# Summing the taps of a shift convolution and joining filter spectra with accumulating transfers

## The chip, the cores and the metric

The kernel runs on one core of a Trainium2 chip. The metric is the device time of one execution in microseconds (us). The core has five instruction queues that matter here: TensorE (PE) for matrix products, VectorE (DVE), ScalarE (ACT), GpSimd (POOL) and SyncE (SP), which only issues transfers. Each works through its own instructions in order and waits on semaphores that other engines and transfers raise. POOL issues transfers too, in a queue of its own.

## What is computed

S = 2048 positions, D = 640 channels, F = 1536. With x = A_q, the reference comes down to this:

```
g  = sigmoid(sum(x * gate_w))                                   # one gate per position
ks = sum over t < 4 of  k_pad[:, t:t+S, :] * shift_k[:, 3-t]    # shift convolution: 4 taps
kv = ks * v
y  = irfft(rfft(kv, 2S) * rfft(ssm_k, 2S))[:S] + kv * ssm_D     # long convolution per channel
a  = q * y
h  = layernorm(x);  u = gelu(einsum("bsd,sf->bdf", h, w1) + b1)
b  = transpose(einsum("bdf,fs->bds", u, w2) + b2)               # MLP over the positions
out = g * a + (1 - g) * b
```

## The kernel before

**The long convolution** is done in P = 4 blocks of 512 positions. Each block of the filter is turned to the time-by-channel layout (`w_time`), transformed to a spectrum `W0..W3` by products with cosine and sine tables on PE (`w_freq`), and evicted from PSUM by ACT with a scale. A spectrum has 9 rows of 640 columns: rows 0 to 3 and 5 to 8 are the cosine and sine parts of four groups of frequencies (`fi`), row 4 holds a copy for the frequency at the edge (`w_nyq`, L1008). Neighbouring spectra are joined (`w_comb`, L998): W_i becomes W_i plus W_(i-1) in frequency groups 2 and 3, and W_i minus W_(i-1) in groups 0 and 1, by two DVE operations over 2560 columns each. Each of the blocks of kv (`kvb`) is folded (`a_split`, into `es`) and transformed into `A0..A3` (`a_freq`). Output block m_ is the sum over j of A_j times W_(m_-j) (`pair`, on DVE, in `Z` with `tT` as scratch), followed by the inverse transform on PE with the table `TI` (`inverse`) and by `epilogue`, which turns half of it round with the matrices `flip` and `flipn`, multiplies by q and the gate and adds the MLP's part.

**The shift convolution** works on tiles of 128 positions, four to a block (`kv_two`). A tile `k4` holds four shifted copies of k side by side, 4 x 640 columns, loaded by one transfer from SP. DVE multiplies it by `shkb`, the taps spread over all partitions (one operation, 2560 columns). PE sums the four products with 4 x 2 accumulating matmuls against the identity, or against `flip` for the two tiles of a block that are stored turned round; ACT evicts the sum to `kvb` and DVE multiplies it by v. For the two turned tiles v is first turned by PE and evicted by ACT. There are four buffers for k4 and five for v.

**The MLP** runs on PE beside this: 384 matmuls `h,w` for the first layer, in blocks of 16 and 32 that hold a PSUM slot, and 384 `gT,w` for the second. Its weights come in pieces by transfers that POOL issues (`w1_load`, `w2_load`). A piece may be loaded only when PE has finished with the buffer's last contents, and for that POOL waits. There are four PSUM slots.

**What sets the order.** Nothing is issued as it is written. Each operation is recorded in a plan with a cost, its reads and writes, and a priority number; `_Plan.run` (L384) then takes, for whichever engine can start earliest, the ready operation of best priority, and this gives the order of each engine's queue. For a transfer the plan uses bytes over a rate and 2 us. `_Tracker` (L18) puts in the waits. So a change of an operation, its engine or its planned cost can move any other operation, and an engine's queue, once set, is kept. Lines named in the profile are mostly those of helpers: L290 every matmul, L676 DVE's two-input operations, L718 ACT's operations, L258 every transfer.

In the function lines, the parts that matter: `dma` (L722) records a transfer, `_Tracker.dma` (L246) issues it; `kv_tile` is L1027, `a_freq` L1043, `tabs` L1111, `inverse` L1114, and the calls in their order are from L1171.

Of the kernel before, what the change touches and what calls it, by code (L numbers as in the profile page):

```python
# [8 lines left out]
BF16 = mybir.dt.bfloat16  # L9
F32 = mybir.dt.float32  # L10
I32 = mybir.dt.int32
ACT = mybir.ActivationFunctionType
# [5 lines left out]
class _Tracker:  # L18
# [227 lines left out]
    def dma(self, stream, out_ap, in_ap, semname, noncontig=False, accum=False):  # L246
        reads = [in_ap]
        writes = [out_ap]
        acc = self.pre(stream, reads, writes)
        engobj = self.eng[stream]  # L250
        sem = self.dma_sems[semname]
        if accum:
            ins = engobj.dma_start(out_ap, in_ap, accum_op=ALU.add)
        elif noncontig:
            with self.nc.allow_non_contiguous_dma(reason="tiny"):
                ins = engobj.dma_start(out_ap, in_ap)
        else:
            ins = engobj.dma_start(out_ap, in_ap)  # L258
        ins.then_inc(sem, 16)
        self.dma_cnt[semname] += 16  # L260
        v = self.dma_cnt[semname]
        self.dma_hist[(semname, v)] = dict(self.known[stream])
        src = ("dma", semname, v)
        for reg, mode in acc:
            self.add_record(reg, mode, src)
        return v
# [250 lines left out]
def _build(nc, A_q, A_k, A_v, A_shift_k, A_ssm_k, A_ssm_D, B_x, B_w1, B_b1, B_w2, B_b2, gate_w, out):  # L517
# [15 lines left out]
    with ExitStack() as es:  # L533
# [14 lines left out]
        def buf(name, shape, dtype, t0, t1):  # L548
            spec.append((name, list(shape), dtype, t0, t1))
# [35 lines left out]
        buf("AFc", [128, 1024], BF16, 0, 90)  # L585
        buf("AFs", [128, 1024], BF16, 0, 90)
        buf("TI", [128, 2, 4, n // 2], BF16, 0, END)
        buf("h", [128, NT, D], BF16, 0, 80)
        groups = [[0], [1]] + [[t, t + 1] for t in range(2, NT, 2)]
        for i in range(2):  # L590
# [83 lines left out]
        def tt(out_, in0, in1, op, pr, eng="DVE"):  # L674
            c = 0.07 + nel(out_) / 1920.0 if eng == "DVE" else 0.3 + nel(out_) / 500.0
            return vop(eng, c, lambda e: e.tensor_tensor(out_, in0, in1, op), [in0, in1], [out_], pr)  # L676
# [16 lines left out]
        def memset(ap, val, pr, eng="POOL"):  # L693
            return vop(eng, 0.3 + nel(ap) / 2000.0, lambda e: e.memset(ap, val), [], [ap], pr)

        def act(out_, in_, func, pr, bias=None, scale=None, accum=None, ps=(), after=()):
            kw = {}
            rr = [in_]
            k = 0
            if bias is not None:  # L700
                kw["bias"] = bias
                if isinstance(bias, bass.AP):
                    rr.append(bias)
                    k += 1
            if scale is not None:
                kw["scale"] = scale
                if isinstance(scale, bass.AP):
                    rr.append(scale)
                    k += 1
            ww = [out_]  # L710
            if accum is not None:
                kw["accum_out"] = accum
                ww.append(accum)
            c = 0.17 + nel(out_) / 1150.0 + 0.09 * k + (0.2 if accum is not None else 0)

            def f(e):
                src = in_() if callable(in_) else in_
                return e.activation(out_, src, func, **kw)  # L718

            return vop("ACT", c, f, rr, ww, pr, ps=ps, after=after)  # L720

        def dma(out_ap, in_ap, semname, pr, stream="SP", noncontig=False):  # L722
            if semname not in T.dma_sems:
                T.add_dma_sem(semname, es.enter_context(nc.semaphore(f"d_{semname}")))
            tot = mybir.dt.size(out_ap.dtype)
            for st, ct in list(out_ap.ap):
                tot *= ct

            def emit():
                T.dma(stream, out_ap, in_ap, semname, noncontig=noncontig)  # L730

            return plan.add(stream, 1.2 if stream == "POOL" else 0.5, emit, [in_ap], [out_ap], pr, dma=max(tot, 20000) / 1e6)

        def pe(pslist, mms, pr, after=()):
            reads = []
# [11 lines left out]
        def two(p_):  # L747
            return lambda: pp[p_.slot][:, :].rearrange("p (c f) -> p c f", c=2)[:, :, 0:HD]
# [4 lines left out]
        def h2(ap):  # L753
            return ap.rearrange("p (c f) -> p c f", c=2)
# [200 lines left out]
        def w_freq(i, pr):  # L955
            osrc = b[f"wT{i}"]
            W = b[f"W{i}"]
            for fi in ORD:
                for c in range(2):
                    p_ = transform(b[f"ee{i % 2}"], osrc, fi, c, pr)  # L960
                    act(h2(W[:, 5 * c + fi, :]), two(p_), ACT.Copy, 1, scale=c_w if fi == 3 else 2.0 / N2, ps=[p_])

        for i in range(P):
            w_time(i)
# [32 lines left out]

        def w_comb(i, pr):  # L998
            W, V = b[f"W{i}"], b[f"W{i - 1}"]


            def half(t, f):
                return bass.AP(tensor=t, offset=f * D, ap=[[9 * D, 128], [5 * D, 2], [1, 2 * D]])

            tt(half(W, 2), half(W, 2), half(V, 2), ALU.add, pr)
            tt(half(W, 0), half(W, 0), half(V, 0), ALU.subtract, pr)

        def w_nyq(i):  # L1008
            W = b[f"W{i}"]
            dma(W[:, 4, :], W[:, 3, :], f"wn{i}", 17)  # L1010
            dma(W[0:1, 4, :], W[0:1, 8, :], f"wn{i}", 17)
            memset(W[0:1, 8, :], 0.0, 2)

        def kv_load(t, pr):
            nm = f"k4_{t % KR}"
# [11 lines left out]
        def kv_tile(t, pr):  # L1027
            k4 = b[f"k4_{t % KR}"]
            v_ = b[f"v_{t % VR}"][:, :]
            r_ = t % NB  # L1030
            mat = b["ident" if r_ < 2 else "flip"][:, :]
            kb = b[f"kvb{t // NB % KVB}"][:, r_ if r_ < 2 else 5 - r_, :]
            if r_ >= 2:
                p_ = _PS()
                pe([p_], halves(p_, [(mat, v_)]), 1.1)
                act(h2(v_), two(p_), ACT.Copy, 1, ps=[p_])
            tt(k4[:, :, :], k4[:, :, :], b["shkb"][:, :, :], ALU.mult, pr)
            p_ = _PS()
            pe([p_], halves(p_, [(mat, k4[:, j, :]) for j in range(KS)]), 1.1)
            act(h2(kb), two(p_), ACT.Copy, 1, ps=[p_])  # L1040
            tt(kb, kb, v_, ALU.mult, pr - 2)

        def a_freq(j, pr):  # L1043
            A = b[f"A{j}"]
            es_ = b["es0"]
            for fi in ORD:
                for c, tab in ((0, AFc), (1, AFs)):
                    p_ = _PS()
                    e0 = 0 if (fi >= 2) == (c == 0) else 2
                    pairs = [(tf(tab, nb, fi), es_[:, e0 + nb, :]) for nb in range(2)]  # L1050
                    pe([p_], halves(p_, pairs), pr)
                    act(h2(A[:, c, fi, :]), two(p_), ACT.Copy, 1, ps=[p_])

        def kv_two(i):
            for t in range(NB * i, NB * i + NB):
# [52 lines left out]
                act(h2(b[f"o1_{q}"][:, k, :]), two(p_), ACT.Identity, 3, bias=b["c2"][:, sb:sb + 1],  # L1108
                    scale=b["omg"][:, sb:sb + 1], ps=[p_])

        def tabs(c, fi, i):  # L1111
            return TI[:, c, fi, i * 128:(i + 1) * 128]

        def inverse(m_):  # L1114
            Z = b[f"Z{m_ % 2}"]
            res = [_PS() for _ in range(4)]
            part = (((0, 2), (0, 3), (1, 0), (1, 1)), ((1, 2), (1, 3), (0, 0), (0, 1)))
            if z_split(m_):
                for i in range(2):
                    for k, fi in enumerate(ORD):  # L1120
                        mms = []
                        for g in range(2):
                            c = [c_ for c_, f_ in part[g] if f_ == fi][0]
                            for h_ in range(2):
                                mms.append((res[2 * i + g], h_ * 512, HD, tabs(c, fi, i),
                                            Z[:, c, fi, h_ * HD:(h_ + 1) * HD], k == 0, k == 3))
                        pe([res[2 * i], res[2 * i + 1]], mms, 1.0)
            else:
                for i in range(2):
                    for g in (1, 0):  # L1130
                        pairs = [(tabs(c, fi, i), Z[:, c, fi, :]) for c, fi in sorted(part[g], key=lambda x: x[1])]
                        pe([res[2 * i + g]], halves(res[2 * i + g], pairs), 1.0)
            return res

# [56 lines left out]
        ts(b["gg"][:, :], b["gth"][:, :], 0.5, 0.5, ALU.mult, ALU.add, 20, eng="POOL")  # L1191
        ts(b["omg"][:, :], b["gth"][:, :], -0.5, 0.5, ALU.mult, ALU.add, 20, eng="POOL")
        tt(b["c2"][:, :], b["omg"][:, :], b["bf"][:, FT:FT + NT], ALU.mult, 20, eng="POOL")
        for q in range(NO):
            mlp2(q)
        for m_ in range(P):
# [37 lines left out]
```

## Time and profile before

| | us |
|---|---|
| median of 3 runs | 226.09 (223.95 to 227.66) |
| span of the profiled execution, first to last instruction | 222.4 |
| PE busy | 202.8 |
| DVE busy | 201.8 |
| ACT busy | 139.9 |
| POOL busy | 41.5 |
| transfers: 39.88 MB, mean over the span | 179 GB/s |

The page gives no time of its own for the profiled execution beside its span; the span is 3.7 us below the runs' median. Busy times count the instructions' own time; an engine that waits isn't busy, and issuing transfers doesn't count for SP. Matmuls overlap, so that the mean of one in the groups is its time from start to end and more than it costs PE. A transfer's "us to landing" runs from its issue to its semaphore.

Stages, by the order of time: filter transforms until about 45 us on PE, with the layernorm's statistics on DVE; from 42 to 126 us the tap products, their sums, the first MLP layer and the first output blocks; from 153 us the second MLP layer on PE beside the last two blocks of `pair` on DVE, the last of which ends at 210.

### The profile page before, as it was taken

Reading aid. Unit: us, or ns where it says so; the run is one execution under the profiler, and the core shown is the slowest. Engines: PE = TensorE matmul, PEld = TensorE weight load, DVE = VectorE, ACT = ScalarE, POOL = GpSimd, SP = SyncE. Lnnn points to the kernel's source line nnn. Section 1 sums busy time; section 2 is a strip of 40 time slices with the busy share of each in tenths; the row PEclk is TensorE's granted clock in tenths of the full one; section 3 lists DMA queues with packets and bytes.
Section 4 is the critical chain, followed back from the end, with each engine's and each line's share of the span. In section 5 each row is a group of like instructions: output and inputs, shape, how many; then the busy total and the mean of one; then the engine's idle time right before and its main releaser. Section 6 shows DMA issues by size and latency. Waiting matters only on the chain.

```text
span 222.4 us, 3751 instructions
## 1 busy us (share of the span) xinstructions
PE 202.8 (91%) x1481; PEld 141.1 (63%) x1481; DVE 201.8 (91%) x253; ACT 139.9 (63%) x221; POOL 41.5 (19%) x79
## 2 busy tenths in 40 slices
PE   0829799999998998999999999999999999999991
PEld 0725547567675774777777777667777777767651
DVE  3379999899988998999999999999999999999771
ACT  4899988997579869683746511799431845432251
POOL 8563330301131010015171010000101101110000
PEclk9988999999999999999999999999999999999997
DMA  6999996139915894899962114302065845286003
GB/s 180 359 325 349 235 298 244 43 109 304 347 41 146 297 391 160 287 295 294 288 181 58 36 16 140 119 3 59 0 202 169 244 116 180 83 253 200 0 3 118
DMA packets 22087, 39.88 MB, mean 179 GB/s; under 512 B 1715, under 2 KB 17205, under 8 KB 22069
## 3 DMA queue, kind: packets, MB, share of 16 engines
q1 hardware_dynamic: 18964, 28.10, 39.8%
q0 software_dynamic: 3104, 11.54, 17.9%
q8 instruction: 12, 0.20, 0.4%
q14 instruction: 7, 0.05, 0.1%
HBM read 36.35 MB, written 2.62 MB: 175 GB/s over the span
## 4 chain that ended last, share of the span: by engine, by line
PE 60%; DVE 22%; ACT 11%; DMA 5%; issue 1%; DVEq 0%; SPq 0%
PE pp L290 60%; DVE Z L676 10%; DVE tT L676 7%; DMA k<-in_A_k_dram 3%; ACT wT L718 2%; ACT W L718 2%; DMA wnat<-in_A_ssm_k_dram 2%; ACT L718 1%; DVE es L676 1%; DVE cg L676 1%; ACT kvb L718 1%; DVE kvb L676 1%; DVE k L676 1%; DVE xg L676 1%; ACT TFs L718 1%
## 5 line engine op out<-in xcount | busy, mean ns | idle before, releaser
L290 PE MATMUL pp<-h,w 128*128 128x320 bf16 x384 | 54.9, 299 | 0.0
L290 PE MATMUL pp<-gT,w 128*128 128x320 bf16 x384 | 53.1, 299 | 0.0
L676 DVE TENSOR_TENSOR tT<-A,W 128x640 bf16<-128x640 bf16 (+4 forms) x44 | 48.0, 1121 | 0.3
L676 DVE TENSOR_TENSOR Z<-Z,tT 128x2560 bf16<-128x2560 bf16 (+3 forms) x35 | 47.1, 1370 | 0.1
L290 PEld LDWEIGHTS pp<-gT,w 128*128 128x128 bf16 x384 | 37.5, 98 | 14.8 <-issue 0.3
L290 PEld LDWEIGHTS pp<-h,w 128*128 128x128 bf16 x384 | 37.5, 98 | 14.6
L258 POOL DMA_DIRECT2D w<-in_B_w_dram x18 | 17.3, 962 | 117.7 <-PE pp L290 117.1
L718 ACT ACTIVATE o<-pp,c,omg 128x640 bf16<-128x640 f32 x16 | 14.2, 884 | 31.4 <-PE pp L290 31.4
L676 DVE TENSOR_TENSOR k<-k,shkb 128x2560 bf16<-128x2560 bf16 x16 | 23.4, 1485 | 0.6 <-DMA k<-in_A_k_dram 0.5
L718 ACT ACTIVATE A<-pp 128x640 bf16<-128x640 f32 x32 | 20.0, 717 | 2.0 <-PE pp L290 2.0
L718 ACT ACTIVATE gT<-pp,bf 128x640 bf16<-128x640 f32 x12 | 9.5, 792 | 18.3 <-PE pp L290 18.2
L290 PE MATMUL pp<-Z,TI 128*128 128x320 bf16 x128 | 18.4, 299 | 1.1 <-ACT kvb L718 1.1
L718 ACT ACTIVATE W<-pp 128x640 bf16<-128x640 f32 x24 | 15.9, 707 | 3.9 <-PE pp L290 3.8
L290 PE MATMUL pp<-ident,wnat 128*128 128x128 bf16 x80 | 8.0, 274 | 10.1 <-DMA wnat<-in_A_ssm_k_dram 5.4
L290 PEld LDWEIGHTS pp<-Z,TI 128*128 128x128 bf16 x128 | 12.4, 98 | 6.4 <-ACT kvb L718 1.4
L718 ACT ACTIVATE kvb<-pp 128x640 bf16<-128x640 f32 x16 | 11.2, 701 | 5.8 <-PE pp L290 5.8
L290 PEld LDWEIGHTS pp<-ident,wnat 128*128 128x128 bf16 x80 | 6.6, 124 | 11.2 <-DMA wnat<-in_A_ssm_k_dram 5.8
L893 DVE BATCH_NORM_STATS2 stats<-xs 128x6 f32<-128x320 bf16 x32 | 13.3, 475 | 0.0
L718 ACT ACTIVATE xg<-xg 128x640 bf16<-128x640 bf16 x16 | 11.6, 734 | 1.7 <-DVE xg L676 1.7
L676 DVE TENSOR_TENSOR Z<-A,W 128x5120 bf16<-128x5120 bf16 x4 | 11.3, 2819 | 0.7 <-ACT A L718 0.7
L290 PE MATMUL pp<-wT,TFc 128*128 128x320 bf16 x48 | 10.1, 300 | 1.7 <-ACT W L718 1.7
L290 PE MATMUL pp<-es,AFs 128*128 128x320 bf16 x64 | 10.1, 300 | 0.8 <-ACT gT L718 0.8
(92 smaller groups left out, 279.2 us busy)
## 6 DMA issues: line engine op xcount, KB each, us to landing
k<-in_A_k_dram SPq DMA_DIRECT2D x15, 640.0 KB, 7.7
w<-in_B_w_dram POOLq DMA_DIRECT2D x8, 768.0 KB, 5.8
w<-in_B_w_dram POOLq DMA_DIRECT2D x10, 512.0 KB, 6.1
wnat<-in_A_ssm_k_dram SPq DMA_DIRECT2D x4, 640.0 KB, 6.5
v<-in_A_v_dram SPq DMA_DIRECT2D x16, 160.0 KB, 7.4
xg<-in_A_q_dram SPq DMA_DIRECT2D x8, 320.0 KB, 7.1
xe<-in_A_q_dram SPq DMA_DIRECT2D x8, 320.0 KB, 3.1
out_dram<-cg SPq DMA_DIRECT2D x8, 320.0 KB, 4.3
```

What stands on the lines that cost most here:

```text
L258: ins = engobj.dma_start(out_ap, in_ap)
L290: ins = self.nc.tensor.matmul(ps_ap, lhsT=lhsT, rhs=rhs, start=start, stop=stop)
L676: return vop(eng, c, lambda e: e.tensor_tensor(out_, in0, in1, op), [in0, in1], [out_], pr)
L718: return e.activation(out_, src, func, **kw)
L893: vop("DVE", 0.41, (lambda o_, i_: lambda e: e.bn_stats(o_, i_))(o_, i_), [i_], [o_], pr)
```

## The change

Taps: the four products of a tile are no longer summed by PE. Two transfers within SBUF, issued by POOL, add columns 1280 to 2559 onto 0 to 1279 (320 KB), and then 640 to 1279 onto 0 to 639 (160 KB); the second waits for the first. DVE multiplies the sum by v; for turned tiles the product, not v, is turned by PE and evicted by ACT.

Spectra: each join is two accumulating transfers of 640 KB from POOL, which add all four groups of W_(i-1) to W_i. So that a sum does for the difference too, the spectra with odd i are evicted with a negative scale in groups 0 and 1, as are the A_j with odd j, and the inverse of odd blocks uses a negated copy of the table, `TIn`, made by POOL. The clearing of half a row in `w_nyq` goes from POOL to DVE. The plan counts an accumulating transfer's bytes 2.5 times.

```diff
-            ins = engobj.dma_start(out_ap, in_ap, accum_op=ALU.add)
+            ins = engobj.dma_start(out_ap, in_ap, accum_op=ALU.add, max_dma_last_dim=2560)
...
+        buf("TIn", [128, 2, 2, n // 2], BF16, 84, END)
...
-        def dma(out_ap, in_ap, semname, pr, stream="SP", noncontig=False):
+        def dma(out_ap, in_ap, semname, pr, stream="SP", noncontig=False, accum=False):
...
+            size = max(tot, 20000) / 1e6 * (2.5 if accum else 1.0)
+            return plan.add(stream, 1.2 if stream == "POOL" else 0.5, emit, [in_ap], [out_ap], pr, dma=size)
...
-                    act(h2(W[:, 5 * c + fi, :]), two(p_), ACT.Copy, 1, scale=c_w if fi == 3 else 2.0 / N2, ps=[p_])
+                    sc = c_w if fi == 3 else (-2.0 / N2 if fi < 2 and i % 2 else 2.0 / N2)
+                    act(h2(W[:, 5 * c + fi, :]), two(p_), ACT.Copy, 1, scale=sc, ps=[p_])
...
-            tt(half(W, 2), half(W, 2), half(V, 2), ALU.add, pr)
-            tt(half(W, 0), half(W, 0), half(V, 0), ALU.subtract, pr)
+            for c in range(2):
+                dma(W[:, 5 * c:5 * c + 4, :].rearrange("p (u f) d -> p u (f d)", u=2),
+                    V[:, 5 * c:5 * c + 4, :].rearrange("p (u f) d -> p u (f d)", u=2),
+                    f"wj{i}_{c}", pr, stream="POOL", accum=True)
...
-            memset(W[0:1, 8, :], 0.0, 2)
+            memset(W[0:1, 8, :], 0.0, 2, eng="DVE")
...
-            if r_ >= 2:
-                p_ = _PS()
-                pe([p_], halves(p_, [(mat, v_)]), 1.1)
-                act(h2(v_), two(p_), ACT.Copy, 1, ps=[p_])
             tt(k4[:, :, :], k4[:, :, :], b["shkb"][:, :, :], ALU.mult, pr)
-            p_ = _PS()
-            pe([p_], halves(p_, [(mat, k4[:, j, :]) for j in range(KS)]), 1.1)
-            act(h2(kb), two(p_), ACT.Copy, 1, ps=[p_])
-            tt(kb, kb, v_, ALU.mult, pr - 2)
+            nm = f"ka_{t % KR}"
+            dma(k4[:, 0:2, :].rearrange("p j d -> p (j d)"), k4[:, 2:4, :].rearrange("p j d -> p (j d)"),
+                nm, pr, stream="POOL", accum=True)
+            dma(k4[:, 0, :], k4[:, 1, :], nm, pr, stream="POOL", accum=True)
+            if r_ < 2:
+                tt(b[f"kvb{t // NB % KVB}"][:, r_, :], k4[:, 0, :], v_, ALU.mult, pr - 2)
+            else:
+                kb = b[f"kvb{t // NB % KVB}"][:, 5 - r_, :]
+                tt(v_, k4[:, 0, :], v_, ALU.mult, pr - 2)
+                p_ = _PS()
+                pe([p_], halves(p_, [(b["flip"][:, :], v_)]), 1.1)
+                act(h2(kb), two(p_), ACT.Copy, 1, ps=[p_])
...
+                    sc = {"scale": -1.0} if fi < 2 and j % 2 else {}
+                    act(h2(A[:, c, fi, :]), two(p_), ACT.Copy, 1, ps=[p_], **sc)
...
-        def tabs(c, fi, i):
-            return TI[:, c, fi, i * 128:(i + 1) * 128]
+        def tabs(c, fi, i, m_):
+            t = b["TIn"] if fi < 2 and m_ % 2 else TI
+            return t[:, c, fi, i * 128:(i + 1) * 128]
...
+        ts(b["TIn"][:, :, :, :], TI[:, :, 0:2, :], -1.0, None, ALU.mult, None, 6, eng="POOL")
```

What the built program of the changed kernel holds, by its queues: 38 accumulating transfers on POOL (32 for taps, 6 for joins), 128 matmuls fewer on PE, six joins fewer on DVE, 16 evictions fewer on ACT. The order differs on every queue. On SP the first k tiles stand ahead of the layernorm's input. On PE the filter transforms come first without interruption, then 96 matmuls of the first MLP layer, then the first turned products. On POOL the second-tap transfers of the second block stand among the first layer's weight loads, and the second layer's weight loads stand behind all taps.

More of the change, by code (lines that the diff above doesn't have):

```diff
@@ L729, in emit @@
             def emit():
-                T.dma(stream, out_ap, in_ap, semname, noncontig=noncontig)
-            return plan.add(stream, 1.2 if stream == "POOL" else 0.5, emit, [in_ap], [out_ap], pr, dma=max(tot, 20000) / 1e6)
+                T.dma(stream, out_ap, in_ap, semname, noncontig=noncontig, accum=accum)
+            size = max(tot, 20000) / 1e6 * (2.5 if accum else 1.0)
+            return plan.add(stream, 1.2 if stream == "POOL" else 0.5, emit, [in_ap], [out_ap], pr, dma=size)
         def pe(pslist, mms, pr, after=()):
@@ L999, in w_comb @@
             W, V = b[f"W{i}"], b[f"W{i - 1}"]
-            def half(t, f):
-                return bass.AP(tensor=t, offset=f * D, ap=[[9 * D, 128], [5 * D, 2], [1, 2 * D]])
-            tt(half(W, 2), half(W, 2), half(V, 2), ALU.add, pr)
-            tt(half(W, 0), half(W, 0), half(V, 0), ALU.subtract, pr)
+            for c in range(2):
+                dma(W[:, 5 * c:5 * c + 4, :].rearrange("p (u f) d -> p u (f d)", u=2),
+                    V[:, 5 * c:5 * c + 4, :].rearrange("p (u f) d -> p u (f d)", u=2),
+                    f"wj{i}_{c}", pr, stream="POOL", accum=True)
         def w_nyq(i):
@@ L1030, in kv_tile @@
             r_ = t % NB
-            mat = b["ident" if r_ < 2 else "flip"][:, :]
-            kb = b[f"kvb{t // NB % KVB}"][:, r_ if r_ < 2 else 5 - r_, :]
-            if r_ >= 2:
-                p_ = _PS()
-                pe([p_], halves(p_, [(mat, v_)]), 1.1)
-                act(h2(v_), two(p_), ACT.Copy, 1, ps=[p_])
-            tt(k4[:, :, :], k4[:, :, :], b["shkb"][:, :, :], ALU.mult, pr)
-            p_ = _PS()
-            pe([p_], halves(p_, [(mat, k4[:, j, :]) for j in range(KS)]), 1.1)
-            act(h2(kb), two(p_), ACT.Copy, 1, ps=[p_])
-            tt(kb, kb, v_, ALU.mult, pr - 2)
+            tt(k4[:, :, :], k4[:, :, :], b["shkb"][:, :, :], ALU.mult, pr)
+            nm = f"ka_{t % KR}"
[7 more added lines that the diff above has]
+                tt(v_, k4[:, 0, :], v_, ALU.mult, pr - 2)
+                p_ = _PS()
+                pe([p_], halves(p_, [(b["flip"][:, :], v_)]), 1.1)
+                act(h2(kb), two(p_), ACT.Copy, 1, ps=[p_])
         def a_freq(j, pr):
@@ L1051, in a_freq @@
                     pe([p_], halves(p_, pairs), pr)
-                    act(h2(A[:, c, fi, :]), two(p_), ACT.Copy, 1, ps=[p_])
+                    sc = {"scale": -1.0} if fi < 2 and j % 2 else {}
+                    act(h2(A[:, c, fi, :]), two(p_), ACT.Copy, 1, ps=[p_], **sc)
         def kv_two(i):
@@ L1124, in inverse @@
                             for h_ in range(2):
-                                mms.append((res[2 * i + g], h_ * 512, HD, tabs(c, fi, i),
+                                mms.append((res[2 * i + g], h_ * 512, HD, tabs(c, fi, i, m_),
                                             Z[:, c, fi, h_ * HD:(h_ + 1) * HD], k == 0, k == 3))
@@ L1130, in inverse @@
                     for g in (1, 0):
-                        pairs = [(tabs(c, fi, i), Z[:, c, fi, :]) for c, fi in sorted(part[g], key=lambda x: x[1])]
+                        pairs = [(tabs(c, fi, i, m_), Z[:, c, fi, :]) for c, fi in sorted(part[g], key=lambda x: x[1])]
                         pe([res[2 * i + g]], halves(res[2 * i + g], pairs), 1.0)
```

## The prediction

> **What bounds the kernel now.** I read the page's busy shares first, then the waits of each engine, then VectorE's and TensorE's order of time, last the transfers.
>
> ```profile
> span 222.4 us, 3751 instructions
> PE 202.8 (91%) x1481; PEld 141.1 (63%) x1481; DVE 201.8 (91%) x253; ACT 139.9 (63%) x221; POOL 41.5 (19%) x79
> PE   0829799999998998999999999999999999999991
> DVE  3379999899988998999999999999999999999771
> ```
>
> PE and DVE (VectorE) are both full: from 31 to 210 us DVE hardly stops, and PE hardly from 18 to 218. The chain of waits gives PE 60% and DVE 22%. So neither has room for a wait, and relief of one alone is worth little.
>
> ```profile
> L676 DVE TENSOR_TENSOR W<-W,W 128x2560 bf16<-128x2560 bf16 x6 | 8.9, 1488 | 0.2
> L290 PE MATMUL pp<-k,ident 128*128 128x320 bf16 x64 | 9.4, 299 | 0.0
> L290 PE MATMUL pp<-k,flip 128*128 128x320 bf16 x64 | 9.3, 299 | 0.0
> L718 ACT ACTIVATE kvb<-pp 128x640 bf16<-128x640 f32 x16 | 11.2, 701 | 5.8 <-PE pp L290 5.8
> L718 ACT ACTIVATE v<-pp 128x640 bf16<-128x640 f32 x8 | 5.4, 704 | 0.9 <-PE pp L290 0.8
> ```
>
> These groups go (kvb keeps 8 of 16). "mean" of a matmul is its latency; it costs PE busy over count, 0.14 us.
>
> ```profile
> POOL w L258 <- PE pp L290: 117.1, 15, 28.0
> POOL vpe L683 <- DVE mv L895: 15.5, 6, 6.7
> POOL W L694 <- DVE W L676: 11.8, 1, 11.8
> POOL W L694 <- DMA W<-W: 6.7, 1, 6.7
> ```
>
> This decides the case. POOL is 19% busy but not free: its queue stands 117 us behind PE, because each weight load there waits until PE has finished with the buffer. Whatever is queued behind such a load waits too. Today nothing urgent is.
>
> ```profile
> k<-in_A_k_dram SPq DMA_DIRECT2D x15, 640.0 KB, 7.7
> w<-in_B_w_dram POOLq DMA_DIRECT2D x8, 768.0 KB, 5.8
> w<-in_B_w_dram POOLq DMA_DIRECT2D x10, 512.0 KB, 6.1
> xe<-in_A_q_dram SPq DMA_DIRECT2D x8, 320.0 KB, 3.1
> W<-W SPq DMA_DIRECT2D x4, 160.0 KB, 7.9
> ```
>
> Median us to landing: 160 KB within SBUF took 7.9 in a busy stage, 320 KB from memory 3.1 in a quiet one.
>
> **The change, part by part**
>
> *Taken away.* DVE: 6 joins x 1.488 = 8.9 us; four memsets of half a row come to it, 0.15 each by the smallest DVE rows. PE: 128 matmuls, 18.7 us. ACT: 16 evictions x 0.70 = 11 us. The sign folded into evictions and into the table TIn costs nothing on ACT (same count of instructions) and none on PE.
>
> *Added on POOL.* 32 accumulating transfers for the taps (320 KB, then 160 KB per tile), 6 for the spectra (640 KB). Issue: w rows took 0.88 to 1.10 us, so about 1 us each. TIn, 1024 elements: 128 elements took 0.57 (flipn), so 4.6 us if it grows with size, 0.6 if not; I take 4. It is queued before one first-tap transfer of batch 2, which has over 10 us to spare, so it is hidden.
>
> *Their landing.* No accumulation is in the trace. Lower bound 3.1 us (xe, quiet). Upper: the 7.9 of W<-W three times, for three passes over the data (read, read, write), 24. I take 6 for a second-tap transfer (nearest to w, the same queue), as it stands behind a w load and a 640 KB join. By the Trainium skill (DMA: Bandwidth & Descriptors, Anatomy of one DMA) a transfer is about 2.0 us plus its bytes at 436 GB/s, an estimate of 2.4 us for 160 KB; by that the sum would be about 4 us less. The trace's 7.9 for a plain 160 KB copy disagrees.
>
> *What is moved.* The planner's new order changes every queue. I walk it on the span's clock, with rates from rows: back to back, a DVE operation takes 1.41 us for 2560 elements, 2.78 for 5120, 0.74 for 1280, 0.41 for 640; 16 matmuls take 2.17 us (102.66 less 100.48), 0.1357 each.
>
> 1. Start. SP now issues the first k tiles ahead of xs, and ACT evicts shkb before the tables (4 x 0.62 = 2.5 us earlier work). ACT's tables and all behind come 3.1 later (0.6 of it the wait for shk, by the 5 us that Dv took to land). DVE takes two k products (2.8) before the statistics and starts these at 19.5, not 14.0. The stretch that took 14.0 to 41.9, with two more k products (2.8), ends at 50.2. The same work with the four products ended at 47.6 before: 2.6 us lost.
> 2. First es. Products with v and two xg take DVE to about 54. Two of them must still be flipped by PE, and these flips now stand behind 96 matmuls of the first MLP (96 x 0.1357 = 13.0 us). The filter transforms come first on PE; ACT's 32 W evictions and 6 tables are 24 us from 22.6 (19.5 before), with 2 us of gaps as now, so PE comes free at 48.5; 61.5 + 0.5 + two evictions of 0.70 gives es at 63.4. DVE idles 9.4. In the kernel before, es came at 56.8, behind joins and k products that covered it.
> 3. A0. es ends at 64.9; eight evictions through two free PSUM slots (the MLP holds the other two) at 0.75 end near 71. DVE has one k product (1.4) to do: idle 4.0, on at 70.3.
> 4. Batch 1. DVE comes to the first tap sum at 82. Its second transfer stands on POOL behind loads that wait for PE's blocks of 32 matmuls (4.34 us each, from 70.2: 74.5, 78.9, 83.2, ...) and behind a join. It is issued at 86 and lands at 92: idle 9.9. Tile 1 is behind one more load (87.6): idle 1.5. Tile 3, behind the load at 91.9, is hidden by DVE's own work. The joins of W1 are issued at 76 and 85 and first wanted near 100: hidden. On SP the copies of W rows (w_nyq) now wait for the joins and stand ahead of batch 2's k loads; these can't start before the sum at 92 frees the buffer, so nothing is lost.
> 5. Batch 2. Its es waits for a flip behind the MLP (1.8), cg for A1's evictions and their flips (3.1). The taps themselves are hidden: the last first-tap is issued at 116, the sum wanted at 136. In batch 3 it is 149 and 164.
> 6. Sum on DVE. From row 54 of its order to the last Z there are 150.0 us of operations: 50.2 + 150.0 + waits (9.4 + 4.0 + 9.9 + 1.5 + 1.8 + 3.1 = 29.7) = 229.9, against 210.0. The tail was 12.4, of which about 2 waited for a last MLP block that is now earlier: 240.3.
> 7. PE's own bound. The first load of the second MLP's weights is now queued on POOL behind all taps and waits for batch 3's first product (160): 161 + 5.8 = 167. Behind it lie 504 matmuls, 68.4 us: 235.4, and about 5 to the end: 240.4. So PE's 18.7 us are not gained; they are idle earlier.
>
> Both ends meet at 240.4. **DMA load** adds to this: between 50 and 100 us the loads are 10.6 MB (nine w of 0.52, four k of 0.66, xg, v, W rows) and the accumulations 4.6 MB. At 286 GB/s (the mean of 70 to 103 us) loads alone take 37 us, accumulations 16 at plain cost and 48 at three passes, in 50 us. At the peaks of 380 the plain case fits. I add 3.6, toward the plain end since the peaks show room: **span 244**. The page has no time of its own for the profiled execution; its span is 3.7 below the runs' median 226.09 (1.6 to 5.3 below the three). So **248 us**.
>
> **The rivals**
>
> *The waits are hidden (faster).* Place: PE's start on the first MLP. If PE reached it at 39 rather than 48.5, steps 2 and 4 would vanish, as flips and weight releases follow PE: 244 less 9.4, 9.9, 1.5, the knock-on 1.8 and 3.1, and the DMA share 3.6 = 214.7, so 218 us. It decides from about 41 us on. For it: PE sheds 18.7 us and is continuous. Against: these matmuls went from after 45 us, and ACT's 24 us of evictions stand before.
>
> *Even.* Half of the waits come: 240.4 - 15 = 225, so 229 us, the saved joins paid back. For it: my landing times in step 4 may be too long; against: step 2 needs no transfer.
>
> *Accumulation is slow.* With payload at 120 GB/s (about 2.5 times the bytes of a copy) a tile's two take 4.1 us and a join 5.5; the queue of step 4, full from 76 us, delivers tile 0 at 103 and the weights as late: 11 us more, 259. From 13 us for both tap transfers of a tile on, batch 3 stalls too, then 270 and beyond. For it: the stage is already 0.85 busy.
>
> *TIn holds DVE.* A POOL row of 16 elements, c<-omg,bf, took 2.67 us beside a DVE product of 2.8, so the two hinder each other. If DVE is the one held, 4 us of TIn go onto DVE: 252. There POOL was the slow one, hence the small chance. The Trainium skill (SBUF — State Buffer, Who interferes with whom) says that a DVE operation with two SBUF inputs contends with a POOL one that reads SBUF and that whichever issues second is blocked; that row agrees.
>
> *The change doesn't do what it says*: the built queues hold the 38 transfers and lack the matmuls, so no.
>
> **How the numbers follow.** Chances: forecast 0.50 (its own range 236 to 256), slow accumulation 0.25, TIn 0.08, hidden 0.09, even 0.08. Within 2% (221.6 to 230.6) is about what a measurement can't tell from no change. Faster 0.09; same 0.08; slower 0.83. The range leaves out the hidden case, the even one and the end of the slow one: 232 to 268.
>
> **What would show it.** Right: DVE idle before es (about 9 us near 54 to 63) released by ACT; DVE kvb waiting on DMA k near 82 to 92; PE idle before the first gT,w near 160; no idle on DVE before kvb in batches 2 and 3; DVE busy about 193. Wrong: PE on its first h,w before 42; accumulations landing over 10 us (slow), or DVE as dense as before (hidden).

## The result and the profile after

The changed kernel took **262.18 us** (median of 4 runs, 261.21 to 264.07); the kernel before, run beside it, 225.09. The ratio is 1.1645, with a 95% interval of 1.1561 to 1.1729. The profiled execution spans 261.3 us. Some executions of a kernel run one or two per cent longer than its others, at a lower granted clock: the medians in this document are of all runs, the ratios of the others alone, and where the profile itself is of such an execution, the table of the experiments gives no busy time for it. The change is slower, as forecast, and the time lies inside the range; it lies outside the likeliest case's own range (236 to 256).

First the page of the changed kernel: busy time of each engine, then the span in 40 slices of 6.5 us, then the software queue that carries POOL's transfers.

```profile
PE 197.2 (75%) x1353; PEld 131.6 (50%) x1353; DVE 197.3 (75%) x251; ACT 130.4 (50%) x205; POOL 91.3 (35%) x114
PE   1949979899699748689940048705999998999990
DVE  5325999980453211899969999999969989999955
PEclk9999999999999999999996555975799999999997
DMA  6999997799999999997079968908005715746102
q0 software_dynamic: 9344, 23.33, 39.6%
```

Both engines do less work than before (PE 197.2 for 202.8, DVE 197.3 for 201.8) and both are idle for a quarter of the span. The slices show where: DVE is hollow from the 10th to the 16th, and PE from the 21st to the 28th, with a fuller stretch between, where the clock granted to it falls to half as well for most of the time. The hollows don't overlap. The view by windows says it in microseconds: the stretch, its length, busy time of each engine (with its instructions), granted clock, share of the DMA engines, GB/s. (The share of 1.06 that the second view gives for the DMA engines is read as full.) First the kernel before:

```profile
50.00:110.00 60.00, 57.69 (x422) 40.23 (x420) 56.76 (x56) 44.48 (x82) 10.21 (x14) 1.00 0.79 259
120.00:180.00 60.00, 59.70 (x439) 42.27 (x438) 59.83 (x46) 31.96 (x47) 4.01 (x5) 1.00 0.36 107
```

and the same stretches of the kernel after:

```profile
50.00:110.00 60.00, 48.38 (x342) 32.24 (x343) 24.57 (x40) 29.76 (x55) 26.10 (x31) 1.00 1.06 267
120.00:180.00 60.00, 28.51 (x171) 17.17 (x168) 57.13 (x48) 22.61 (x34) 30.57 (x20) 0.74 0.67 163
```

Before, PE and DVE (third busy figure) worked side by side, 58 and 57 of 60 us. After, they work in turn: from 50 to 110 us DVE does 24.6 us of work, 32.2 less than before; from 120 to 180 DVE is full and PE, which has little left to do but what DVE hands it, does 28.5. The 32 us that DVE loses in the first stretch are most of the 37 by which the kernel is slower.

What DVE waited for there, from the timeline of the kernel after (start, duration, operation, in brackets the idle time ahead and what ended it):

```profile
66.56 1.56 DVE L677 TENSOR_TENSOR es<-kvb 128x1280 bf16<-128x1280 bf16 x2 [7.99 <-ACT kvb L719]
73.55 1.56 DVE L677 TENSOR_TENSOR tT<-A,W 128x1920 bf16<-128x1920 bf16 x2 [4.03 <-ACT A L719]
85.79 1.49 DVE L677 TENSOR_TENSOR k<-k,shkb 128x2560 bf16<-128x2560 bf16 x1 [1.74 <-DMA k<-in_A_k_dram]
92.34 0.33 DVE L695 MEMSET W<- 1x320 uint32 x1 [5.06 <-DMA W<-W]
95.98 0.82 DVE L677 TENSOR_TENSOR xg<-xg,gwb 128x1280 bf16<-128x1280 bf16 x1 [3.31 <-DMA xg<-in_A_q_dram]
100.14 0.82 DVE L677 TENSOR_TENSOR xg<-xg,gwb 128x1280 bf16<-128x1280 bf16 x1 [3.33 <-DMA xg<-in_A_q_dram]
105.72 0.33 DVE L695 MEMSET W<- 1x320 uint32 x1 [4.76 <-DMA W<-W]
106.08 2.83 DVE L677 TENSOR_TENSOR Z<-A,W 128x5120 bf16<-128x5120 bf16 x1
108.82 0.48 DVE L677 TENSOR_TENSOR kvb<-k,v 128x640 bf16<-128x640 bf16 x1
```

The first two waits are those of the prediction's steps 2 and 3. Then come waits for loads (k and xg) in a stretch in which the DMA engines are full, and two clearings of half a row (`w_nyq`) that wait for joins. The clearing at 105.72 is that of W0: it may happen only when the last join, which reads W0, is done. Behind it stands the first spectral product Z, at 106.08; before, it came at 63.34. The tap sum at 108.82, on which step 4 turned, had no wait of its own.

The transfers behind this, from the list of issues (KB each, median us from issue to landing):

```profile
w<-in_B_w_dram POOLq DMA_DIRECT2D x10, 512.0 KB, 11.9
k<-k POOLq DMA_DIRECT2D x16, 320.0 KB, 5.5
W<-W POOLq DMA_DIRECT2D x6, 640.0 KB, 12.9
k<-k POOLq DMA_DIRECT2D x16, 160.0 KB, 6.1
```

The weights took 6.1 before. And PE's side of the second stretch:

```profile
149.88 0.71 PE L290 MATMUL pp<-v,flip 128*128 128x320 bf16 x2 [15.52 <-DVE v L677]
176.69 0.72 PE L290 MATMUL pp<-v,flip 128*128 128x320 bf16 x2 [8.78 <-DVE v L677]
180.88 6.08 PE L290 MATMUL pp<-gT,w 128*128 128x320 bf16 x24 [1.27 <-DMA w<-in_B_w_dram]
```

PE waits for turned products that DVE makes late, and the second layer's `gT,w` starts at 180.88 (152.74 before).

### The profile page after: what moved, and what is told of

The parts are those of the page before. It is cut to its first block, busy times and chain, and to the rows that moved or that the text cites. A ratio compares the mean times of both kernels' runs of the same rounds, so it can differ in the third digit from the quotient of the medians.

```text
span 261.3 us, 3508 instructions
## 1 busy us (share of the span) xinstructions
PE 197.2 (75%) x1353; PEld 131.6 (50%) x1353; DVE 197.3 (75%) x251; ACT 130.4 (50%) x205; POOL 91.3 (35%) x114
## 3 DMA queue, kind: packets, MB, share of 16 engines
q0 software_dynamic: 9344, 23.33, 39.6%
## 4 chain that ended last, share of the span: by engine, by line
PE 31%; DMA 28%; DVE 24%; POOL 10%; ACT 4%; issue 3%; DVEq 0%; POOLq 0%; ACTq 0%
PE pp L290 31%; DMA w<-in_B_w_dram 14%; DMA k<-in_A_k_dram 6%; POOL c L677 5%; DMA out_dram<-cg 5%; DVE stats L895 5%; DVE k L677 4%; DVE Z L677 4%; DVE tT L677 3%; DMA k<-k 3%; DVE cg L677 2%; DVE h L685 1%; DVE idx L684 1%; DVE ee L677 1%; POOL k L253 1%
## 5 line engine op out<-in xcount | busy, mean ns | idle before, releaser
L290 PE MATMUL pp<-h,w 128*128 128x320 bf16 x384 | 53.8, 299 | 9.1 <-DMA w<-in_B_w_dram 8.7
L290 PE MATMUL pp<-gT,w 128*128 128x320 bf16 x384 | 56.2, 308 | 2.9 <-DMA w<-in_B_w_dram 2.5
L253 POOL DMA_DIRECT2D k<-k x32 | 31.8, 1234 | 36.4 <-DVE k L677 28.5
L290 PE MATMUL pp<-v,flip 128*128 128x320 bf16 x16 | 4.5, 381 | 27.6 <-DVE v L677 27.6
L290 PEld LDWEIGHTS pp<-v,flip 128*128 128x128 bf16 x16 | 1.1, 104 | 30.3 <-DVE v L677 30.1
L290 PE MATMUL pp<-es,AFc 128*128 128x320 bf16 x64 | 12.0, 343 | 5.7 <-DVE es L677 5.6
L290 PE MATMUL pp<-ident,wnat 128*128 128x128 bf16 x80 | 9.4, 309 | 9.2 <-DMA wnat<-in_A_ssm_k_dram 5.4
L290 PE MATMUL pp<-Z,TI 128*128 128x320 bf16 x96 | 15.9, 306 | 0.0
L290 PEld LDWEIGHTS pp<-ident,wnat 128*128 128x128 bf16 x80 | 7.7, 139 | 10.9 <-DMA wnat<-in_A_ssm_k_dram 5.4
L677 DVE TENSOR_TENSOR xg<-xg,gwb 128x1280 bf16<-128x1280 bf16 x8 | 6.5, 818 | 8.5 <-DMA xg<-in_A_q_dram 8.5
## 6 DMA issues: line engine op xcount, KB each, us to landing
w<-in_B_w_dram POOLq DMA_DIRECT2D x10, 512.0 KB, 11.9
W<-W POOLq DMA_DIRECT2D x6, 640.0 KB, 12.9
```

What stands on the lines that cost most here:

```text
L253: ins = engobj.dma_start(out_ap, in_ap, accum_op=ALU.add, max_dma_last_dim=2560)
L290: ins = self.nc.tensor.matmul(ps_ap, lhsT=lhsT, rhs=rhs, start=start, stop=stop)
```

## The experiments

I began with two readings: the transfers cost the time (their bytes load the DMA engines and land late), or the order does (what stands behind what on the queues, which the planner makes anew). The letters of the theories are not the same throughout the expectations. In `copies`, `weight1`, `joins_only` and `taps_only`, A is the transfers and B the order. In all others B is the load of the transfers; C, D and E are named where they come up. Each text says in words what it bears on. The medians, with DVE's busy time in the window from 50 to 110 us:

| kernel | us | ratio to before | DVE of 60 us |
|---|---|---|---|
| before (beside these runs 224.8 to 225.9) | 225.1 | 1 | 56.8 |
| after | 262.2 | 1.1645 (1.1561 to 1.1729) | 24.6 |
| copies | 253.3 | 1.1304 (1.1213 to 1.1395) | 32.4 |
| tiny | 250.3 | 1.1136 (1.1084 to 1.1189) | 34.9 |
| weight1 | 257.4 | 1.1496 (1.1415 to 1.1578) | 27.4 |
| joins_only | 251.3 | 1.1187 (1.1069 to 1.1305) | 30.8 |
| taps_only | 239.5 | 1.0647 (1.0528 to 1.0767) | |
| noclear | 253.8 | 1.1299 (1.1243 to 1.1354) | 35.1 |
| nyq_joins | 249.8 | 1.1111 (1.1058 to 1.1163) | 39.4 |
| nyq_after | 262.6 | 1.1674 (1.1629 to 1.1719) | 30.6 |
| inplace_joins | 247.8 | 1.0947 (1.0877 to 1.1017) | 30.8 |
| swap_joins | 252.6 | 1.1108 (1.0993 to 1.1222) | |
| before_rate | 225.2 | 0.9899 (0.9793 to 1.0006) | |
| after_unchained | 269.8 | 1.192 (1.1809 to 1.2031) | |

**What the bytes cost, in one order.** `copies` and `tiny` keep the changed kernel's order on every queue. In `copies` the 38 transfers copy and don't add, so the sums are left out. The parameter `max_dma_last_dim` goes with the addition, and the software queue moves the same 23.33 MB in 6016 packets and not 9344.

```diff
-            ins = engobj.dma_start(out_ap, in_ap, accum_op=ALU.add, max_dma_last_dim=2560)
+            ins = engobj.dma_start(out_ap, in_ap)
```

> The 38 accumulating transfers move the same bytes by the same routes and in the same order as plain copies (the sums are left out, everything else is computed). Theory A (the cost of accumulating itself: two trips of data where a copy has one, so that the transfer engines are full from 55 to 109 us): the 4.6 MB accumulated in that stage took about 24 us at the 190 GB/s seen when accumulations run alone, as copies at 350 to 400 GB/s 12 us; the first tap product of batch 2 then comes near 97 instead of 108.8 us, and the time falls by about 12 us to 250. Theory B (the order on POOL and PE: taps behind weight loads, flips behind the MLP): the queues are the same, so 262 within 2 us.

In `tiny` the plan sees the whole transfers and what is issued are 64 or 128 elements per partition (the second tap sum in the same way):

```diff
-                T.dma(stream, out_ap, in_ap, semname, noncontig=noncontig, accum=accum)
+                T.dma(stream, *(small or (out_ap, in_ap)), semname, noncontig=noncontig, accum=accum)
...
-                    f"wj{i}_{c}", pr, stream="POOL", accum=True)
+                    f"wj{i}_{c}", pr, stream="POOL", accum=True,
+                    small=(W[:, 5 * c + 3, 0:64], V[:, 5 * c + 3, 0:64]))
...
-                nm, pr, stream="POOL", accum=True)
+                nm, pr, stream="POOL", accum=True, small=(k4[:, 0:2, 0:64], k4[:, 2:4, 0:64]))
```

> The changed kernel with the order of every queue kept, but each of the 38 accumulating transfers moves 64 or 128 elements per partition rather than 640 to 2560, so nearly all of the sums are left out of the computation; each still is issued and waited for at its place. Theory C (joins stand late on POOL's queue, behind weight loads, and the last one releases the first product): the clearing of W0 still comes at 92 to 97, since its last join is issued there, and the time is 238 to 248 us. Theory B (bytes on the DMA engines): their cost is gone, 225 to 235 us. That the new order alone costs the time, whatever the transfers do: 255 us or more.

Measured 253.3 and 250.3. So with the order held, adding instead of copying is worth 262.2 - 253.3 = 8.9 us (theory A expected 12, with the tap sum of 108.82 near 97, and it came at 100.70; B expected none; how much of the 8.9 is the greater number of packets is not shown), the copies' bytes another 3.0, and **all bytes together 11.9 us**. The other 25 us stay when the transfers move next to nothing. They are not all order for certain, since 38 nearly empty transfers are still a load: the software queue took 22.6% of the 247.6 us in `tiny`, 56 us, against 40 us before. The result of `tiny` fell between the cases that were expected (238 to 248 by theory C, which is explained below, and 255 by the order).

The landing times went with it. Here are issues of `copies`, in the same order, for the 5.5, 12.9 and 11.9 us of the kernel after; the 160 KB of the second tap sums landed in 2.9 us there, in 6.1 in the kernel after:

```profile
k<-k POOLq DMA_DIRECT2D x16, 320.0 KB, 4.0
W<-W POOLq DMA_DIRECT2D x6, 640.0 KB, 7.1
w<-in_B_w_dram POOLq DMA_DIRECT2D x10, 512.0 KB, 7.6
```

DVE's timeline in `tiny`:

```profile
66.49 1.56 DVE L677 TENSOR_TENSOR es<-kvb 128x1280 bf16<-128x1280 bf16 x2 [7.85 <-ACT kvb L719]
73.48 1.56 DVE L677 TENSOR_TENSOR tT<-A,W 128x1920 bf16<-128x1920 bf16 x2 [4.02 <-ACT A L719]
92.31 0.33 DVE L695 MEMSET W<- 1x320 uint32 x1 [6.22 <-DMA W<-W]
92.67 2.83 DVE L677 TENSOR_TENSOR Z<-A,W 128x5120 bf16<-128x5120 bf16 x1
```

and POOL's, with the issue of the last join that releases this:

```profile
83.60 2.43 POOL L253 DMA_DIRECT2D k<-k  x2
87.01 0.91 POOL L258 DMA_DIRECT2D w<-in_B_w_dram  x1 [0.97 <-PE pp L290]
87.91 0.94 POOL L253 DMA_DIRECT2D W<-W  x1
```

The waits for es and A0 are the same to 0.14 us: no transfer is in them. The first Z comes at 92.67 instead of 106.08 because the last join lands 4.4 us after its issue and not 16.7; but it is issued at 87.91 in any case, behind weight loads that wait for PE.

**What the planner's price does.** `weight1` plans an accumulation at its bytes, not 2.5 times them; only the order changes.

```diff
-            size = max(tot, 20000) / 1e6 * (2.5 if accum else 1.0)
+            size = max(tot, 20000) / 1e6 * (1.0 if accum else 1.0)
```

> The changed kernel with a planned weight of 1 for the bytes of an accumulating transfer instead of 2.5: the same work, another order on every queue; on PE the turned products are no longer behind 96 matmuls of the MLP, on POOL the taps stand ahead of more of the weight loads. Theory A: the same bytes have to pass in the same stage, 255 to 265 us. Theory B: the waits at the first es (8 us) and part of those at batch 2 go, 235 to 250 us.

257.4: another order, 5 us less, inside the range of theory A and outside that of B. DVE's waits became others (14.4 us for xg, 14.0 for tap sums of the turned tiles).

**One half at a time.** `joins_only` sums the taps on PE as before; `taps_only` joins on DVE as before, without negative scales and TIn and with the clearing on POOL. The diffs are the two halves of the change; the core of each, undone:

```diff
-            dma(k4[:, 0:2, :].rearrange("p j d -> p (j d)"), k4[:, 2:4, :].rearrange("p j d -> p (j d)"),
-                nm, pr, stream="POOL", accum=True)
+            pe([p_], halves(p_, [(mat, k4[:, j, :]) for j in range(KS)]), 1.1)
```

```diff
-                    f"wj{i}_{c}", pr, stream="POOL", accum=True)
+            tt(half(W, 2), half(W, 2), half(V, 2), ALU.add, pr)
+            tt(half(W, 0), half(W, 0), half(V, 0), ALU.subtract, pr)
```

> Only the joins of spectra are accumulating transfers; the taps are summed on PE as before. Theory A: 3.9 MB at 190 GB/s are 21 us of transfer time in a stage of some 55 us where the engines were 0.63 to 0.86 busy, about what is free: 219 to 230 us, with waits on DMA in that stage. Theory B: nothing urgent stands behind or beside a join, so 216 to 222, the DVE's 8.9 us gained in part, PE being the other bound.

> Only the taps are summed by accumulating transfers; the joins stay on DVE. Theory A: two thirds of the accumulated bytes are left, but only 2 MB of 4.6 in the crowded stage: 240 to 250 us. Theory B: every tap still waits on POOL among the weight loads and the flips on PE behind the MLP: 252 to 262, and no gain from the joins' leaving the transfer engines.

Joins alone cost 26 us and taps alone 14, 40.6 together, where the whole change costs 37.1. The taps came out just below theory A's range (240 to 250). The joins were a surprise to both readings: six transfers, which relieve DVE of 8.9 us, cost more than the 32 of the taps. `joins_only` also has the negative scales, the clearings on DVE and `TIn`; these are small there, as the clearings take 0.33 us each and PE's waits for `TIn` come to 1.4 us.

**Is it the clearing of W0?** From the wait at 105.72 I formed a theory C: the first Z waits for the last join by way of the clearing. `noclear` leaves it out for W0, `nyq_joins` and `nyq_after` do the edge rows before the joins and then join 9 rows, so that W0 is final at once.

For `noclear`:

```diff
-            memset(W[0:1, 8, :], 0.0, 2, eng="DVE")
+            if i:
+                memset(W[0:1, 8, :], 0.0, 2, eng="DVE")
```

For the other two, in which `max_dma_last_dim` also rises from 2560 to 3200:

```diff
-                dma(W[:, 5 * c:5 * c + 4, :].rearrange("p (u f) d -> p u (f d)", u=2),
+                r0, r1 = ((0, 4), (4, 9))[c]
+                dma(W[:, r0:r1, :].rearrange("p f d -> p (f d)").rearrange("p (u x) -> p u x", u=2),
...
+        for i in range(P):
+            w_nyq(i)
         w_comb(3, 17.0)
         w_comb(2, 17.0)
         w_comb(1, 17.0)
-        for i in range(P):
-            w_nyq(i)
```

> Joins alone by accumulating transfers (taps on TensorE as before), and the clearing of half a row of W0 is left out, which leaves one frequency of one spectrum wrong. The transfers move the same bytes. Theory C (the first spectral product waits for that clearing, and the clearing for the last join, which reads W0): the first product Z, 5120 elements, comes near 65 to 70 rather than at 105.65, and 251.3 falls to 228 to 238 us. Theory B (the transfers' load on the DMA engines costs the time): nothing is taken off the DMA engines, so 246 to 254 us.

> Joins alone; the edge row of each spectrum is copied and half a row cleared before the joins, and the joins add all 9 rows (1.47 MB each rather than 1.31), so W0 is final before any join and nothing is left out of the result. Theory C: as without the clearing, 228 to 238 us, with the first product near 65 to 70. Theory B: 12% more bytes in the joins, so 250 to 258 us.

> The changed kernel with the edge rows done before the joins, and joins of 9 rows; taps by transfers as in it. Theory C: the wait of the first product for the last join goes, and of the 26 us that the joins alone cost most comes back: 238 to 248 us against 262.2. Theory B: 258 to 266 us.

The first Z did come early, at 71.64 in `noclear` and 67.21 in `nyq_joins`, against 105.65 in `joins_only`, and at 69.33 in `nyq_after`, against 106.08 in the kernel after. The time didn't follow: 253.8, 249.8 and 262.6. **Theory C fell**, as far as kernels that are planned anew can show it: with that wait gone, another order costs as much. What took the wait's place, in the waits of `nyq_joins` (line, awaited, total us, times, longest):

```profile
PE pp L290 <- POOL TIn L684: 10.6, 1, 10.6
DVE cg L677 <- ACT o L719: 13.6, 2, 10.9
DVE cg L677 <- ACT pb L719: 8.5, 1, 8.5
DVE Z L677 <- ACT A L719: 3.7, 1, 3.7
```

With another order DVE stood before other results of PE and ACT, and from 152 to 179 us first PE stood before TIn and then DVE, for 10.9 us, before what PE made late. The wait that ends last is not what the time hangs on if the next one is as long.

**Order and transfer apart.** Two kernels exchange them. `inplace_joins` is the kernel before in exactly its order, with each join on DVE taken out and an accumulating transfer issued by POOL at that point (all add; the difference in groups 0 and 1 is left out). `swap_joins` is `joins_only` in its order, with DVE adding at the points where the transfers stood.

```diff
-            tt(half(W, 2), half(W, 2), half(V, 2), ALU.add, pr)
-            tt(half(W, 0), half(W, 0), half(V, 0), ALU.subtract, pr)
+            for k, f in enumerate((2, 0)):
...
+                plan.add("DVE", 0.07 + 2560 / 1920.0,
+                         (lambda nm, o_, i_: lambda: T.dma("POOL", o_, i_, nm, accum=True))(nm, half(W, f), half(V, f)),
+                         [half(W, f), half(V, f)], [half(W, f)], pr)
```

and for `swap_joins`, against `joins_only`:

```diff
             def emit():
-                T.dma(stream, out_ap, in_ap, semname, noncontig=noncontig, accum=accum)
+                if accum:
+                    T.op("DVE", lambda e: e.tensor_tensor(out_ap, out_ap, in_ap, ALU.add), [out_ap, in_ap], [out_ap])
+                else:
+                    T.dma(stream, out_ap, in_ap, semname, noncontig=noncontig, accum=accum)
```

> The kernel before, in exactly its order on every queue, except that each of its six join operations on VectorE is taken out and an accumulating transfer of the same 640 KB is issued by POOL at that point of the order; all of them add, so the difference in groups 0 and 1 is left out of the computation. Theory D (what costs the time is the order that the planner makes once the transfers are in the plan): 218 to 232 us, since the order stays and VectorE sheds 8.9 us. Theory B (the transfers themselves, their landing times and bytes): near the 251.3 of the joins alone, 245 us or more.

> The mirror of it: the kernel with the joins alone by transfers, in its order on every queue, but each transfer is taken out and VectorE adds the same 2560 columns at that point of the order. No accumulating transfer is left. Theory D: the order remains, so 245 to 262 us. Theory B: the transfers are gone, 222 to 232 us.

| | joins on DVE | joins by transfer |
|---|---|---|
| order of before | 225 | 247.8 (ratio 1.09) |
| order of joins_only | 252.6 (ratio 1.11) | 251.3 (ratio 1.12) |

Neither reading holds alone: **either change by itself costs 22 to 27 us, and both together no more.** `inplace_joins` came out as theory B said, `swap_joins` as D. In the old order the transfers stall the chip. POOL's timeline in `inplace_joins`:

```profile
50.00 1.29 POOL L253 DMA_DIRECT2D W<-W  x1 [7.76 <-ACT W L718]
61.22 1.19 POOL L253 DMA_DIRECT2D W<-W  x1 [9.93 <-DMA W<-W]
67.76 1.19 POOL L253 DMA_DIRECT2D W<-W  x1 [5.35 <-DMA W<-W]
73.92 0.62 POOL L694 MEMSET W<- 1x640 bf16 x1 [4.97 <-DMA W<-W]
75.33 0.94 POOL L258 DMA_DIRECT2D w<-in_B_w_dram  x1 [0.32 <-issue]
```

The joins are a chain: W3 must have read W2 before W2's own join may change it, and W2 must have read W1. On DVE a link took 1.49 us; here the links took 11.2, 6.5 and 6.2, and POOL, waiting for each, held back the weight load behind them, which went out at 55.74 before and now at 75.33. DVE's Z lines paid 19.7 us for it (groups of `inplace_joins`: busy and mean, then idle ahead and what ended it):

```profile
L676 DVE TENSOR_TENSOR Z<-A,W 128x5120 bf16<-128x5120 bf16 x4 | 11.3, 2821 | 19.7 <-DMA W<-W 12.5 <-POOL W L694 7.2
```

The planner knows of such landing times and puts other work ahead; the order that it finds costs as much even when DVE does the joins. Where that order loses can be read from the first half of `joins_only`, here two lines of PE and four of DVE:

```profile
54.12 9.94 PE L290 MATMUL pp<-h,w 128*128 128x320 bf16 x72 [0.34 <-ACT kvb L719]
89.33 4.51 PE L290 MATMUL pp<-h,w 128*128 128x320 bf16 x32
72.02 1.56 DVE L677 TENSOR_TENSOR tT<-A,W 128x1920 bf16<-128x1920 bf16 x2 [4.16 <-ACT A L719]
95.76 0.49 DVE L677 TENSOR_TENSOR kvb<-kvb,v 128x640 bf16<-128x640 bf16 x1 [10.79 <-issue]
105.29 0.33 DVE L695 MEMSET W<- 1x320 uint32 x1
105.65 2.83 DVE L677 TENSOR_TENSOR Z<-A,W 128x5120 bf16<-128x5120 bf16 x1
```

PE takes 72 matmuls of the MLP in one go before it begins A0, where the kernel before gave them in eights and sixteens between its small products, and DVE waits for A0. The first tap products of the third block are ready at 85.0, but PE takes 64 more of the MLP, among the products for A1, and sums them from 93.68 on: DVE stands 10.8 us before this sum, which ACT has evicted at 95.66 ("issue" is a wait whose cause the profile doesn't show). `swap_joins` has both waits too, of 7.7 and 8.0 us, though no accumulating transfer is left in it. And the clearing ahead of the first Z has no idle time before it in `joins_only`, while `swap_joins` has that Z at 108.01: in this order Z is late by its place in DVE's queue, and not by the last join.

**Is any new order as bad?** `before_rate` plans the kernel before with another rate for all transfers.

```diff
-    DMA_RATE = 0.30
+    DMA_RATE = 0.27
```

> The kernel before, with one constant of the planner changed: it takes 0.27 rather than 0.30 MB per us for every transfer. The same operations, engines and transfers, in another order. If the order of the kernel before is one that nearly any change of the plan loses (theory D in its strong form): 235 to 250 us. If only plans with dear accumulations are bad, or the order does not matter: 221 to 230 us.

225.2, and a ratio of 0.99 whose interval reaches 1: no difference that is clear. So it isn't that only one order is good; the bad orders seen here came with accumulations in the plan.

**Without the chain.** The last run takes rows of h, finished early, as the source of the joins in the changed kernel, so the spectra are wrong and nothing is chained.

```diff
-                    V[:, 5 * c:5 * c + 4, :].rearrange("p (u f) d -> p u (f d)", u=2),
+                    b["h"][:, 0:4, :].rearrange("p (u f) d -> p u (f d)", u=2),
```

> The changed kernel, joins and taps by transfers, but each join adds rows of h, which are finished early, onto W_i instead of rows of W_(i-1): the same bytes, wrong spectra, and no chain from W3 over W2 to W1, neither on the chip nor in the plan. Theory E (the joins form a chain, since a spectrum must be read by its neighbour's join before its own join may change it; by transfers each link takes 6 to 11 us, on VectorE 1.5, and both the waits and the planner's order put off what hangs on it): what the joins cost goes, what the taps cost stays, so it comes near the 239.5 of the taps alone: 234 to 246 us against 262.2. Theory B (bytes and landing times of the transfers): 256 to 264 us.

269.8, worse than with the chain and outside both ranges, so the expectation failed. It decides less than I wanted: the planner's order moved at the start too, with tiles of k ahead of the filter's `wnat` blocks on SP's queue and the layernorm's input ahead of three of the four, and that is likely a loss of its own. That the chain costs time is seen in `inplace_joins`; that taking it away would mend the changed kernel is not shown. Open is also which of the planner's choices makes its orders bad in general: the blocks of MLP matmuls ahead of the small products are seen in the kernel after (96 before its first turned products) and in `joins_only`, but no run puts them back alone. None of these kernels beats the one before by more than its interval.

## Why the prediction was right in the large and where it failed

The sign and the range held; the account was 14 us short (248 against 262.2), outside its own case's range. That the time lies inside the wide range is in part luck: the upper part was put there for slow accumulation, and most of the loss came another way. Against the prediction's clock:

| | predicted | measured | late by |
|---|---|---|---|
| step 1, row 54 of DVE | 50.2 | 55.4 | 5.2 |
| step 2, es | 63.4 | 66.6 | 3.2 |
| step 3, on after A0 | 70.3 | 73.6 | 3.3 |
| step 4, first tap sum of batch 1 | 92 | 108.8 | 16.8 |
| step 6, last Z ends | 229.9 | 250.4 | 20.5 |
| end of the span | 240.3, with the load term 244 | 261.3 | 17.3 |

- **Step 1** left out a wait of 5.88 us for the first tiles of k.
- **Steps 2 and 3** were right in cause and nearly in size (9.4 and 4.0; 8.0 and 4.0), and `tiny` shows that they belong to the order, not to any transfer.
- **Step 4 failed**, and with it most of the miss is made: 13.5 of the 21.0 us by which the span passes the 240.3 of the steps (17.3 of these are left when the load term, which belongs to the same stretch, is added). "The joins of W1 are issued at 76 and 85 and first wanted near 100: hidden." The issues were at 79.3 and 89.1, near enough. But I looked for who wants the new W1 and forgot who must wait until the old W0 is read: the clearing of W0, moved by the same diff to DVE, ahead of the first Z. And the last join took 16.7 us to land. The tap transfer, my own cause for that idle time, ended no wait there, though the four second-tap transfers issued from 89 to 103 us took 14.0 us to land (median), not 6. `nyq_after` adds that mending this one wait brings nothing back (262.6), so the failure is not one wait but the cover: DVE's work from 50 to 110 us hung on PE's small products, on loads and on joins, all late at once.
- **Step 5** named 1.8 and 3.1 us; there was one wait of 2.3 for cg before 140, and the taps of batches 2 and 3 were hidden as said (0.46 us).
- **Step 7** was right in its mechanism. `gT,w` started at 180.9, not 167, since batch 3's first product came late. From there PE needed 74.5 us to its end at 255.4, 68.4 predicted; the difference is the halved clock and short waits. Both ends met again, as forecast. DVE's busy time came to 197.3 us and not about 193, as each clearing took 0.33 us, not 0.15, and a few operations ran longer.
- **The load term** was mis-sized: 3.6 us added, where the bytes of the transfers are worth 11.9 by `tiny` (landing times included). The guess "toward the plain end" was wrong, since adding instead of copying is 8.9 of them.
- **The rivals.** "Slow accumulation" gave 259, nearest to the result, and its sign, joins landing in over 10 us, was there (12.9); but its place, the taps' queue, was not, and by `tiny` only 12 of the 37 us are the transfers' bytes. So it is near by its number alone. "Hidden" and "even" are out. "TIn holds DVE" is out: TIn took 4.0 us, and of DVE's operations beside it one of 2560 elements took 2.31 instead of 1.47 us.

## What to carry to other kernels

When two engines are both at nine tenths, ask of a change not only what each sheds but what keeps each busy at every moment: here both shed work and the kernel lost 37 us, since they came to work in turn. A join in place is also a reader of its neighbour, and when an instruction of 1.5 us became a transfer, each link of that chain took 6 to 11 us; list who must wait for the old value to be read, not only who wants the new one. To learn what a stall is worth, take it out with the order of the queues held: the last-ending wait, and a chain's share, named losses here that did not come back.

## What the runs showed of the hardware that was not expected

Accumulating cost the DMA engines about twice what copying did, packets as they were cut included. For the same 23.33 MB in the same order the software queue took 39.6% of 16 engines' time over 261.3 us, 103 us, in 9344 packets, and 28.7% of 251.3 us, 72 us, in the 6016 packets of `copies`; the kernel before, without the 38 transfers, took 40 us. If the weight loads took those 40 in all three, that leaves 64 us against 32. In the median an accumulation of 320 KB landed in 5.5 us, of 160 KB in 6.1 and of 640 KB in 12.9; the copies in 4.0, 2.9 and 7.1.

The granted clock follows PE's idleness. Here are three lines of the changed kernel's PE, the first behind 3.4 us of idle time after the 15.5 shown above:

```profile
157.96 4.45 PE L290 MATMUL pp<-es,AFc 128*128 128x320 bf16 x16 [3.42 <-DVE es L677]
162.20 2.46 PE L290 MATMUL pp<-es,AFs 128*128 128x320 bf16 x16
225.86 20.04 PE L290 MATMUL pp<-gT,w 128*128 128x320 bf16 x144
```

The first 16 took 4.24 us to the start of the next, 0.27 each, the next 16 2.46 and, long after, 144 in a row 20.04, 0.14 each. Over these three stretches the granted clock was 0.50, 0.95 and 1.00. The mean clock from 120 to 180 us was 0.74, where the kernel before had 1.00 (the windows above). The Trainium skill (TensorE: Matmul & The Clock Gate, What's actually happening) says that an idle window of about 3.4 us halves the clock and about 3.4 us of work restores it; these rows agree in kind, with 15.5 us of idle time before and 4.2 us of work until the clock was back, but none of them isolates 3.4 us.

A POOL operation that reads SBUF can take very long beside a dense DVE. TIn took 4.01 us in the changed kernel, where it began in a gap of DVE, and 12.87 in `nyq_joins`, with DVE busy throughout; the operation on 16 elements took 12.23 and ended when DVE paused. It isn't always so: in `nyq_joins` the same operation on 16 elements took 0.33 us, with DVE busy too. From the changed kernel:

```profile
119.19 12.23 POOL L677 TENSOR_TENSOR c<-omg,bf 128x16 f32<-128x16 f32 x1
133.11 4.01 POOL L684 TENSOR_SCALAR TIn<-TI 128x1024 bf16<-128x1024 bf16 x1
```

So POOL is the one that is held for long, as in the trace of before (2.67 us beside a DVE operation of 2.8), and in `nyq_joins` PE waited 10.6 us for it.
